# Front of a two-branch attention kernel: a third tile for branch A's outputs, two tiles for the query copies

## The chip, the cores and the metric

The kernel runs on one core of a Trainium2 chip. The metric is the device time of one execution in microseconds (us), the median over several runs. Engines are named as the profile names them: PE is TensorE (PEld its weight loads), ACT is ScalarE, DVE is VectorE, POOL is GpSimd, SP the engine that issues most DMAs here.

## The reference

Two attention branches over the same input x of 2048 rows and 512 columns, mixed row by row by a gate. Branch A is a sliding window of 8 positions with a step of 2, branch B full attention with one key and value head shared by 32 query heads of 16 columns.

```python
def _A_ref(x, wqkv, wo):          # H = 32, Dh = 16, W, dil = 8, 2
    qkv = (x @ wqkv).reshape(B, S, 3, H, Dh).transpose(2, 0, 3, 1, 4)
    q, k, v = qkv[0], qkv[1], qkv[2]
    idx = pos[:, None] - (jnp.arange(W) * dil)[None, :]
    logits = jnp.einsum("bhsd,bhswd->bhsw", q, kg) * scale   # kg, vg: rows idx of k, v
    attn = softmax(where(idx >= 0, logits, -1e9))
    return jnp.einsum("bhsw,bhswd->bhsd", attn, vg) ... @ wo

def _B_ref(x, wq, wk, wv, wo):
    q, k, v = heads(x @ wq), x @ wk, x @ wv
    p = softmax(jnp.einsum("bhqd,bkd->bhqk", q, k) * (Dh ** -0.5))
    return jnp.einsum("bhqk,bkd->bhqd", p, v) ... @ wo

g = sigmoid((x * gate_w).sum(-1, keepdims=True))
return g * _A_ref(...) + (1 - g) * _B_ref(...)
```

## The kernel before

**Stages.** The first 290 us are the front. It splits x and the weights into a high and a low part (`xh`, `xl`, `wqh`, `wql`, `wah`, `wal`), so that three products of reduced precision stand for one of full precision, and makes branch B's keys and queries and branch A's queries, keys and values. Then follow 16 units of branch B (4 blocks of 512 query rows by 8 groups of 4 heads, taken in 16 pairs), each over 16 key tiles: `exp_pair` makes scores and exponentials, `weighted` multiplies them with the values. Three output phases and a tail project both branches. Branch A's own arithmetic runs on POOL beside the units.

**Lumps.** The front's TensorE work is a list of lumps: query products m = 2 to 15, and 64 products (gg, j) of branch A, four column groups gg by 16 row tiles j. A lump is 12 products (4 chunks of the inner dimension by 3 parts), each cut into two matmuls of 64 rows (`h = slice(64 * b, ...)` in `mm`), one for the lower and one for the upper half of the array; two such matmuls run at once. The banks `fb[0]` to `fb[3]` take the lumps in turn (the last two go to `m1` and `po`).

**Between them** TensorE makes scores of branch B for the row maxima that the exponentials subtract. `fill_diff` (line 401) multiplies the queries with differences of keys (`diff_mm`, line 399) into a bank `pd0` or `pd1`; ACT copies it through a Relu into `dd` or `dd2` (line 411); `fill_sum` (line 419) makes plain scores into `m1` or `po`, and DVE adds the two and takes the maximum (line 423). A bank `pd` is free for the next difference once ACT has copied it.

**After a query lump** `queries_post` (line 217) has ACT copy the bank into `qraw` (line 223), and POOL then makes the high part `qhi` (line 230) and the low part `qlo` (line 231) from that copy. `queries_out` stores both to the scratch `qd` in HBM, and `stack` loads whole units of queries from there into a `qst` tile, both on SP's queue. `qraw` has one buffer in the pool `parts0`.

**After a lump of branch A** `a_post` (line 246) has ACT copy the bank into a stage tile (line 257), two row tiles j to a tile; when the second is in, SP stores the pair (384 KB) to the scratch `ad` (line 265), from where POOL's branch A loads it. With gg = 0 ACT also copies the values and the gate's column (line 259). The stage tiles are taken in turn from the list `stages`. A tile is added while the list has fewer than two or the key `"next"` is set; `done_mm` sets that key once, with the pool `third`, at the first lump of branch A, and the first `a_post` takes it out again. So the list ends with two tiles, `stage0` in the pool `third` and `stage1` in the pool `phase1`.

**What sets the order.** The program is one list of instructions written by Python; running clocks (`clk`) model each engine, `pick` and `front_stream` choose the next matmul by them, and `tasks` hold work with a due time (splits, stores, loads) that `run_tasks` issues when the modelled time is reached. The modelled clocks don't know which buffer an instruction writes: that an engine waits for a buffer is added by the framework, as a semaphore wait on the instruction. Each engine then runs its own instructions in this order, and SP issues its DMAs in this order.

**Memory.** `wkr` holds the key weights, read by `keys` (line 195) for the four key products at the start, in the pool `phase0`, which like `parts0` is given back when the first lump of branch A has begun (`done_mm`). `a_values` (line 595) is part of POOL's branch A: `av` holds a product for one window position, and `tr8`, `tr4`, `tr2` in `a_scores` hold the steps of a tree sum.

Of the kernel before, what the change touches and what calls it, by code (L numbers as in the profile page):

```python
# [6 lines left out]
F32 = mybir.dt.float32  # L7
# [6 lines left out]
P = 128  # L14
# [3 lines left out]
DH = 16  # L18
NJ = S // P
C = D // P  # L20
# [9 lines left out]
AG = 2  # L30
# [10 lines left out]
NH = NJ // 2  # L41
# [7 lines left out]
def gated_mix_kernel(ctx, tc, xt, wa, wk, wq, wo_a, wo_b, out):  # L49
# [36 lines left out]
    def after(eng, ready, dur):  # L86
        clk[eng] = max(clk[eng], ready) + dur
        return clk[eng]
# [4 lines left out]
    p0q = tc.alloc_tile_pool(name="parts0", bufs=1, side="right")  # L93
    p0 = tc.alloc_tile_pool(name="phase0", bufs=1, side="right")
# [3 lines left out]
    dd2 = p1.tile([P, 2, 512], F32, name="dd2")  # L98
    wqh = p0.tile([P, C, D], F32R, name="wqh")
    wql = p0.tile([P, C, D], F32R, name="wql")  # L100
    wkr = p0.tile([P, C, P], F32, name="wkr")
    wqr = [t[:, k].rearrange("p (c q) -> p c q", c=C) for t in (wq01, dd) for k in range(2)]
    waraw, wah, wal = {}, {}, {}
    GO = [0, GN + VN, 2 * GN + VN, 3 * GN + VN]
# [104 lines left out]
    def queries_out(m, hi, lo):  # L209
        qb, cc = divmod(m, NHG // 2)  # L210
        for s, src in enumerate((hi, lo)):
            nc.sync.dma_start(qd[s, :, qb, 8 * cc:8 * cc + 8, :], src.bitcast(F32))

    def parts_of():
        return p0q.tile([P, 512], F32R, name="qhi", bufs=3), p0q.tile([P, 512], F32R, name="qlo", bufs=2)

    def queries_post(m, bank, key, ups_at):

        nonlocal pool
        settle("rest", 0)  # L220
        own = p0q.tile([P, 512], F32, name="qraw", bufs=1)
        hi, lo = parts_of()
        got = nc.scalar.activation(own, bank, AF.Copy)
        at = after("act", clk["pe"] + T_LAT, 0.62)
        mark(got, at, ups_at)
        free[key] = at + 0.1

        def rest():
            nonlocal pool
            nc.gpsimd.tensor_copy(hi, own)  # L230
            nc.gpsimd.tensor_sub(lo, own, hi.bitcast(F32))
            pool = max(pool, 1e3 * at) + 2300
            queries_out(m, hi, lo)
            if m > 4 and m % 2 and len(stacked) < NB:
                stack(len(stacked))

        tasks.append((max(pool / 1e3, at), rest, (), "rest"))

    stage, stages, turns = {}, [], [0, 0]
# [6 lines left out]
    def a_post(gg, j, bank, key, ups_at):  # L246

        if j % 2 == 0:
            settle("store", 1)
            if len(stages) < 2 or "next" in stage:  # L250
                stages.append((stage.pop("next", None) or p1).tile([P, GC, 2, AN], F32, name=f"stage{len(stages)}"))
            stage["t"] = stages[turns[1] % len(stages)]
            turns[1] += 1
        st = stage["t"]
        end = gg == C - 1 and j == NJ - 1
        src = bank[:, :GN].rearrange("p (g n) -> p g n", g=GC)
        got = nc.vector.tensor_copy(st[:, :, 1, :], src) if end else nc.scalar.activation(st[:, :, j % 2, :], src, AF.Copy)
        if gg == 0:
            nc.scalar.activation(vst[:, j, 0:DH + 1], bank[:, GN:GN + DH + 1], AF.Copy)
        at = after("dve" if end else "act", clk["pe"] + T_LAT, 0.5 if gg else 0.7)  # L260
        mark(got, at, ups_at)
        free[key] = at + 0.1
        if j % 2 == 1:
            dst = ad[gg * GC:(gg + 1) * GC, HALO:, :].rearrange("g (p j) n -> p g (j n)", j=NJ)
            tasks.append((at + 0.3, lambda: nc.sync.dma_start(dst[:, :, (j - 1) * AN:(j + 1) * AN], st.rearrange("p g j n -> p g (j n)")), (), "store"))
        if j == NJ - 1:
            tasks.append((at + 1.0, whole, (gg,)))
# [21 lines left out]
    def stack(u):  # L289
        qb, hg = divmod(u, NHG)  # L290
        for b in range(2):
            hi, lo = (qd[s, :, qb, 4 * hg + 2 * b:4 * hg + 2 * b + 2, :].rearrange("d c n -> d (c n)") for s in range(2))
            ap = [list(x) for x in hi.ap]
            twice = bass.AP(tensor=hi.tensor, offset=hi.offset, ap=[ap[0], [0, 2]] + ap[1:])
            dst = qst[place(u)].rearrange("p c n -> p (c n)").bitcast(F32)
            nc.sync.dma_start(dst[64 * b:64 * b + 32], twice)
            nc.sync.dma_start(dst[64 * b + 32:64 * b + 48], lo)
        stacked.append(clk["pe"] + (6.8 if pe else 5.0))
# [11 lines left out]
    def mark(inst, end, up=None):  # L310
        marks.append((ups[0] if up is None else up, end, inst.ins.name))
# [220 lines left out]
    oa, p2, woh, wol, p1x = [], [], [], [], []  # L532
# [62 lines left out]
    def a_values(g, hf):  # L595
        lg, e = alog.pop(g), aext.pop(g)
        js = slice(NH * hf, NH * hf + NH)
        lgv = lg.rearrange("p w j h -> p w (j h)")
        nc.gpsimd.tensor_mul(asum[g], asum[g], gate[:, 0, js].unsqueeze(2).to_broadcast([P, NH, AG]))
        nc.gpsimd.tensor_mul(lgv, lgv, asum.pop(g).rearrange("p j h -> p (j h)").unsqueeze(1).to_broadcast([P, W, NH * AG]))  # L600
        yield 850
        ao = oa[g // 8][:, js, g % 8 * AC:(g % 8 + 1) * AC].rearrange("p j (h d) -> p j h d", d=DH)
        for w in range(W):
            o = HALO - DIL * w
            av = p2[0].tile([P, NH, AG, DH], F32, name="av", bufs=1) if w else ao
            nc.gpsimd.tensor_mul(av, e[:, o:o + NH, 2 * AC:].rearrange("p j (h d) -> p j h d", d=DH), lg[:, w].unsqueeze(3).to_broadcast([P, NH, AG, DH]))  # L606
            yield 730
            if w:
                nc.gpsimd.tensor_add(ao, ao, av)  # L609
                yield 830  # L610
# [311 lines left out]
    def settle(kind, n):  # L922
        for task in [t for t in tasks if t[3:] == (kind,)][:-n or None]:
            tasks.remove(task)
            task[1](*task[2])
# [52 lines left out]
    def work():  # L978
# [16 lines left out]
        def values(g, hf):  # L995
            while ("sum", g, hf) not in done:
                if summing:
                    yield lambda: ("exp",) + summing[0] in done
                    yield from sums()
                else:  # L1000
                    yield lambda: ("sum", g, hf) in done
            yield lambda: g < 8 or p2b
            yield from a_values(g, hf)
            if g == NAG - 1:
                done.add(hf)
# [118 lines left out]
    def done_mm(at):  # L1124
# [27 lines left out]
        if lump[0] == "q":  # L1152
            m = lump[1]
            queries_post(m, bank, key, ended_at.pop(x))
            ahead_wa(0, m - 4)
        else:
            gg, j = lump[1:]
            a_post(gg, j, bank, key, ended_at.pop(x))
            if gg + 1 < C:
                ahead_wa(gg + 1, j - 2)  # L1160
# [165 lines left out]
    for x in range(2):  # L1326
        js = slice(2 * x, 2 * x + 2)
        two = four[:, x]
        tt, own = two[:, 0].rearrange("p (b d) -> p b d", d=32), two[:, 1]
# [61 lines left out]
```

## Time and profile before

| | us |
|---|---|
| median of 3 runs (lowest, highest) | 1464.12 (1463.6, 1466.82) |
| the profiled execution | 1463.92 |
| its span, first to last instruction | 1462.1 |
| mean granted clock of TensorE | 0.999 |
| busy: PE, ACT, DVE, POOL | 1448.2, 1292.0, 1141.9, 954.6 |

A row of a timeline has the start and the length in us, the engine, the line, the operation and its tiles (out<-in, without buffer numbers), the shape, and in square brackets the idle time of the engine ahead of it and what ended it. A row of the table of waits has who waited for whom, the total in us, how many times, and the longest. A row of the chain of waits has start, length and what the chain went through. A row of the table by windows has the window, its length, the busy time (and instructions) of PE, PEld, DVE, ACT and POOL, the granted clock of TensorE, the share of the DMA engines and GB/s.

### The profile page before, as it was taken

What the parts mean: (1) busy time and instruction counts of PE and PEld (TensorE: products, weight loads), DVE (VectorE), ACT (ScalarE), POOL (GpSimd) and SP (SyncE); (2) the same over time, 40 slices, a digit from 0 to 9 for tenths busy, and PEclk for the clock granted to TensorE, in tenths of its full rate; (3) what the DMA queues carried; (4) which work ended last, traced back from release to release, by engine and by line L of the source; (5) the groups of instructions that cost most, each with busy time, mean ns of one, the idle gap of its engine ahead of it and who ended that gap; (6) DMA issues with size and microseconds to landing.
All of it is one profiled execution on the core that took longest, in us unless ns stands there. A gap on an engine that the chain in (4) does not pass through costs nothing.

```text
span 1462.1 us, 29622 instructions
## 1 busy us (share of the span) xinstructions
PE 1448.2 (99%) x10989; PEld 743.1 (51%) x10989; DVE 1141.9 (78%) x1857; ACT 1292.0 (88%) x1649; POOL 954.6 (65%) x1714
## 2 busy tenths in 40 slices
PE   9999999999999999999999999999999999999999
PEld 6899999833333333333333373333333743373335
DVE  6888888788887888888888876888888778778821
ACT  5788888699999999999999988999999889879994
POOL 6951888888979898898898897888881211130000
PEclk9999999999999999999999999999999999999999
DMA  6652442411202111012022020211200000000000
GB/s 225 171 159 72 146 129 89 136 49 41 79 12 79 47 44 68 31 39 78 17 74 72 13 93 8 82 42 42 71 12 13 27 16 1 2 31 1 1 2 29
DMA packets 45688, 85.70 MB, mean 59 GB/s; under 512 B 10400, under 2 KB 28248, under 8 KB 41448
## 3 DMA queue, kind: packets, MB, share of 16 engines
q1 hardware_dynamic: 38552, 45.21, 10.0%
q0 software_dynamic: 6560, 37.95, 7.8%
q8 instruction: 86, 1.41, 0.4%
q10 hardware_dynamic: 432, 0.66, 0.1%
q14 instruction: 58, 0.48, 0.1%
HBM read 57.97 MB, written 25.25 MB: 57 GB/s over the span
## 4 chain that ended last, share of the span: by engine, by line
PE 92%; POOL 2%; ACT 2%; DVE 1%; issue 1%; DMA 1%; SPq 0%; POOLq 0%; ACTq 0%; DVEq 0%
PE po L486 34%; PE pe L471 24%; PE pf L1109 9%; PE pm L328 8%; PE ps L328 5%; PE pe L803 5%; PE pd L399 3%; PE po L328 1%; PE pe L1320 1%; ACT pexp L477 1%; DMA ad<-stage 1%; POOL xl L82 1%; DVE mx L350 1%; DMA xraw<-xt 0%; PE pf L195 0%
## 5 line engine op out<-in xcount | busy, mean ns | idle before, releaser
L477 ACT ACTIVATE pexp<-pe 128x1024 f32<-128x1024 f32 x1021 | 983.4, 1023 | 64.4 <-PE pe L471 61.1
L350 DVE TENSOR_REDUCE mx<-pm 128x2 f32<-128x1024 f32 x470 | 574.0, 1221 | 178.1 <-PE pm L328 174.4
L486 PE MATMUL po<-pexp,vst 128*32 128x512 f32 x4096 | 546.4, 605 | 4.5 <-DVE mx L423 3.3
L471 PE MATMUL pe<-qst,kst 64*128 64x512 f32 x1914 | 492.6, 459 | 2.0 <-ACT pexp L477 2.0
L471 PEld LDWEIGHTS pe<-qst,kst 64*128 64x128 f32 x1914 | 193.5, 184 | 437.0 <-ACT pexp L477 408.6
L411 ACT ACTIVATE dd<-pd 128x512 f32<-128x512 f32 x384 | 224.5, 601 | 50.7 <-PE pd L399 24.7
L362 DVE TENSOR_REDUCE mx<-ps 128x1 f32<-128x512 f32 x309 | 209.8, 679 | 3.4 <-PE pe L803 2.0
L328 PE MATMUL ps<-kst,qst 62*128 62x512 f32 x475 | 194.2, 409 | 0.2
L549 POOL TENSOR_TENSOR pr<-aext 128x256 f32<-128x256 f32 x256 | 181.9, 740 | 4.2 <-DMA aext<-ad 4.0
L328 PE MATMUL pm<-kst,qst 62*128 62x512 f32 x880 | 178.7, 397 | 0.5 <-ACT pexp L477 0.2
L609 POOL TENSOR_TENSOR oa<-oa,av 128x256 f32<-128x256 f32 x224 | 164.1, 733 | 15.8
L486 PEld LDWEIGHTS po<-pexp,vst 128*32 128x32 f32 x4096 | 80.6, 108 | 171.7 <-issue 157.2
L423 DVE CUSTOM_DVE_ANT_0 dd<-ps,dd 128x512 f32<-128x512 f32 x193 | 133.0, 689 | 25.8 <-PE ps L328 7.8
L423 DVE CUSTOM_DVE_ANT_0 dd<-po,dd 128x512 f32<-128x512 f32 x191 | 131.6, 689 | 22.6 <-PE po L328 10.2
L1109 PE MATMUL pf<-wal,xh 64*128 64x384 f32 (+1 forms) x496 | 148.3, 337 | 0.0
L399 PE MATMUL pd<-kd,qst 62*128 62x512 f32 x372 | 146.4, 398 | 1.7 <-ACT dd L411 1.7
L606 POOL TENSOR_TENSOR av<-aext,lg 128x256 f32<-128x256 f32 x224 | 139.4, 622 | 12.6
L1109 PE MATMUL pf<-wah,xh 64*128 64x384 f32 (+1 forms) x496 | 145.7, 338 | 0.0
L1109 PE MATMUL pf<-wah,xl 64*128 64x384 f32 (+1 forms) x496 | 142.3, 337 | 0.0
L328 PEld LDWEIGHTS ps<-kst,qst 62*128 62x128 f32 x475 | 87.8, 185 | 33.7 <-DVE mx L362 25.6
L513 POOL TENSOR_TENSOR rl<-rl,gate_t 128x16 f32<-128x16 f32 x31 | 7.1, 230 | 143.3 <-DVE rl L506 143.1
L1109 PEld LDWEIGHTS pf<-wal,xh 64*128 64x128 f32 x496 | 90.7, 186 | 0.3
(210 smaller groups left out, 1817.6 us busy)
## 6 DMA issues: line engine op xcount, KB each, us to landing
aext<-ad POOLq DMA_DIRECT2D x32, 1056.0 KB, 5.4
ad<-stage SPq DMA_DIRECT2D x32, 384.0 KB
qst<-qd SPq DMA_DIRECT2D x60, 128.0 KB
xraw<-xt SPq DMA_DIRECT2D x16, 256.0 KB
qd<-qhi SPq DMA_DIRECT2D x16, 256.0 KB
qd<-qlo SPq DMA_DIRECT2D x16, 256.0 KB
qst<-qd SPq DMA_DIRECT2D x60, 64.0 KB
qst<-ml SPq DMA_DIRECT2D x212, 2.0 KB
```

The lines of the kernel that those rows point to most:

```text
L328: nc.tensor.matmul(dst, qst[place(v)][b:b + 62, pr, t * P:(t + 1) * P], kst[b:b + 62, kc * 512:(kc + 1) * 512], start=True, stop=True)
L350: got = nc.vector.tensor_reduce(m[:, :, pr, t, kc], dst, AX.X, ALU.max)
L362: got = nc.vector.tensor_reduce(m[:, odd, pr, t, kc:kc + 1], dst, AX.X, ALU.max)
L399: nc.tensor.matmul(dst, qst[place(v)][b:b + 62, pr, t * P:(t + 1) * P], kd[0][b:b + 62, kc // 2, :], start=True, stop=True)
L411: got = nc.scalar.activation(held[b][k], dst, AF.Relu)
L423: got = nc.vector.tensor_tensor_reduce(held[b][k], dst, held[b][k], 1.0, -FMAX, ALU.add, ALU.max, m[:, b, pr, t, kc:kc + 1])
L471: nc.tensor.matmul(bank[:, odd, :], kst[b:b + 64, kt * P:(kt + 1) * P], qst[place(u)][b:b + 64, pr, :], start=True, stop=True)
L477: got = nc.scalar.activation(e, bank, AF.Exp, scale=SCALE)
L486: nc.tensor.matmul(po[32 * i:32 * i + 32, :], vst[:, kt, :], pexp[s, i // 2][:, i % 2, :], start=(kt == 0), stop=(kt == NJ - 1))
L549: nc.gpsimd.tensor_mul(pr[:, k], q, e[:, o:o + NH, AC:2 * AC])
L609: nc.gpsimd.tensor_add(ao, ao, av)
L1109: inst = nc.tensor.matmul(home(x)[0][:, :n], l[h], r[h], start=(i == 0 and b == 0), stop=(i == 3 * C - 1 and b == 1))
```

## The change

Three things change place in memory. The list `stages` takes a third tile, `stage2`, in the pool `phase1` (the condition with `"next"` is replaced by a plain count). The copies of even query products go to a tile of their own, `qraw2`, in the memory of `wkr`; the odd ones stay in `qraw`. And `av` shares the memory of `tr4`.

```diff
-    wkr = p0.tile([P, C, P], F32, name="wkr")
+    wkr = p0.tile([P, C, P], F32, name="wkr", tag="wkr", bufs=1)
...
-        own = p0q.tile([P, 512], F32, name="qraw", bufs=1)
+        own = p0q.tile([P, 512], F32, name="qraw", bufs=1) if m % 2 else p0.tile([P, 512], F32, name="qraw2", tag="wkr", bufs=1)
...
-            if len(stages) < 2 or "next" in stage:
+            if len(stages) < 3:
                 stages.append((stage.pop("next", None) or p1).tile([P, GC, 2, AN], F32, name=f"stage{len(stages)}"))
...
-            av = p2[0].tile([P, NH, AG, DH], F32, name="av", bufs=1) if w else ao
+            av = p2[0].tile([P, NH, AG, DH], F32, name="av", tag="tr4", bufs=1) if w else ao
```

Every engine has the same instructions in the same places before and after; what changes is the tile that some of them write, and what they wait for. Two places on ACT's queue show it. In these rows a name carries its number, `dd` and `dd2` are the Relu copies, `pf` the lumps' banks, `DMAHW` a DMA's semaphore, `Pool` POOL's.

The query copies of m = 3 (in `qraw`) and m = 4, with the Relu copies between them, on ACT. Before:

```order
L411 ACTIVATE dd2_122<-pd1_93 128x512 [waits PE_49]
L223 ACTIVATE qraw_426<-pf1_98 128x512 [waits PE_49,Activation_49,Pool_49]
L411 ACTIVATE dd_86<-pd0_92 128x512 [waits PE_49]
L411 ACTIVATE dd_86<-pd1_93 128x512 [waits DVE_49,PE_49]
L411 ACTIVATE dd2_122<-pd0_92 128x512 [waits PE_49]
L411 ACTIVATE dd2_122<-pd1_93 128x512 [waits DVE_49,PE_49]
L411 ACTIVATE dd_86<-pd0_92 128x512 [waits DVE_49,PE_49]
L411 ACTIVATE dd_86<-pd1_93 128x512 [waits DVE_49,PE_49]
L223 ACTIVATE qraw_482<-pf2_99 128x512 [waits PE_49,Activation_49,Pool_49]
```

And after, at the same place on ACT:

```order
L411 ACTIVATE dd2_122<-pd1_93 128x512 [waits PE_49]
L223 ACTIVATE qraw_426<-pf1_98 128x512 [waits PE_49]
L411 ACTIVATE dd_86<-pd0_92 128x512 [waits PE_49]
L411 ACTIVATE dd_86<-pd1_93 128x512 [waits DVE_49,PE_49]
L411 ACTIVATE dd2_122<-pd0_92 128x512 [waits PE_49]
L411 ACTIVATE dd2_122<-pd1_93 128x512 [waits DVE_49,PE_49]
L411 ACTIVATE dd_86<-pd0_92 128x512 [waits DVE_49,PE_49]
L411 ACTIVATE dd_86<-pd1_93 128x512 [waits DVE_49,PE_49]
L223 ACTIVATE qraw2_482<-pf2_99 128x512 [waits PE_49,Activation_49,Pool_49]
```

The copy of m = 3 no longer waits for POOL; that of m = 4 still does, for POOL's work on m = 2 in place of m = 3.

The stage copies of j = 3 and j = 4 of the first column group on ACT. Before:

```order
L257 ACTIVATE stage1_1303<-pf1_98 128x4x96 [waits PE_49]
L259 ACTIVATE vst_72<-pf1_98 128x17
L411 ACTIVATE dd2_122<-pd1_93 128x512 [waits DVE_49,PE_49]
L411 ACTIVATE dd_86<-pd0_92 128x512 [waits DVE_49,PE_49]
L411 ACTIVATE dd_86<-pd1_93 128x512 [waits DVE_49,PE_49]
L411 ACTIVATE dd2_122<-pd0_92 128x512 [waits DVE_49,PE_49]
L257 ACTIVATE stage0_1207<-pf2_99 128x4x96 [waits DMAHW5_49,PE_49,Activation_49]
```

And after, at the same place on ACT:

```order
L257 ACTIVATE stage1_1303<-pf1_98 128x4x96 [waits PE_49]
L259 ACTIVATE vst_72<-pf1_98 128x17
L411 ACTIVATE dd2_122<-pd1_93 128x512 [waits DVE_49,PE_49]
L411 ACTIVATE dd_86<-pd0_92 128x512 [waits DVE_49,PE_49]
L411 ACTIVATE dd_86<-pd1_93 128x512 [waits DVE_49,PE_49]
L411 ACTIVATE dd2_122<-pd0_92 128x512 [waits DVE_49,PE_49]
L257 ACTIVATE stage2_1391<-pf2_99 128x4x96 [waits PE_49]
```

The copy of j = 4 waits for the store of j = 0, 1 before, and for its product alone after. Every later pair waits for the store of three pairs before in place of two. Beyond that, the first stage copy (j = 0) gets a wait for POOL's `qlo` of m = 14, since `stage0` lies in memory that `qraw2`'s pool gives back, and one load of `qstx` on SP's queue a wait for ACT's copy of m = 14. No row of `av` gets a wait.

## The prediction

> **What bounds the kernel now.** I read the page's busy times and chain of waits first, then the front alone (0 to 290 us, all that the change touches), and there who waited for whom.
>
> ```profile
> PE 1448.2 (99%) x10989; PEld 743.1 (51%) x10989; DVE 1141.9 (78%) x1857; ACT 1292.0 (88%) x1649; POOL 954.6 (65%) x1714
> PE 92%; POOL 2%; ACT 2%; DVE 1%; issue 1%; DMA 1%; SPq 0%; POOLq 0%; ACTq 0%; DVEq 0%
> ...
> ACT stage L257 <- DMA ad<-stage: 4.5, 2, 3.0
> ...
> ACT qraw L223 <- POOL qlo L231: 4.4, 4, 2.5
> ...
> PE pd L399 <- ACT dd L411: 1.7, 4, 0.9
> ```
>
> The chain is TensorE for 92%: whatever lets its queue run on is worth its whole length, and an ACT wait is worth only what reaches TensorE through it. ACT waits 4.5 us (two times) for a stage buffer's store and 4.4 us (four times) for POOL to finish with the query copy: 8.9 us in all. Behind them stand the Relu copies `dd` of line 411, and the difference matmuls of line 399 need the bank that such a copy empties. TensorE is shown idle there for 1.7 us in four places. A stall costs more than its idle time, since the modelled ends of matmuls cover part of it, so below I take it from start to start, against the usual step from one pair of half-array matmuls to the next: 0.235 us at 512 columns (63.15 to 63.39 in the rows below), and by the columns 0.18 us for the A products with their 384 or 402.
>
> **The query copies.** With one `qraw`, the copy of query product m waits until POOL has split m-1; now it waits for m-2. The first two rows are ACT's at m=3, the others TensorE's.
>
> ```profile
> 38.80 0.60 ACT L223 ACTIVATE qraw<-pf 128x512 f32<-128x512 f32 x1 [2.49 <-POOL qlo L231]
> 39.29 3.70 ACT L411 ACTIVATE dd<-pd 128x512 f32<-128x512 f32 x6
> ...
> 37.59 0.39 PE L1109 MATMUL pf<-xh,wql 64*128 64x512 f32 x1
> 39.22 0.39 PE L328 MATMUL po<-kst,qst 62*128 62x512 f32 x1
> 39.94 0.50 PE L399 MATMUL pd<-kd,qst 62*128 62x512 f32 x1 [0.33 <-ACT dd L411]
> 40.27 0.40 PE L1109 MATMUL pf<-xl,wqh 64*128 64x512 f32 x1
> ```
>
> The last matmul into m=3's bank ends at 37.59 + 0.39 = 37.98, so the copy can start 0.8 us earlier and the next `dd` can end near 39.1 instead of 39.9. TensorE wants it at 39.22 + 0.235 = 39.46, so the stall goes whole: (39.94 - 39.22 - 0.235) + (40.27 - 39.94 - 0.235) = 0.58 us; the second bracket is the slow restart behind it. The same at m=5 and m=8:
>
> ```profile
> 47.45 0.60 ACT L223 ACTIVATE qraw<-pf 128x512 f32<-128x512 f32 x1 [0.74 <-POOL qlo L231]
> 48.02 0.39 PE L1109 MATMUL pf<-xh,wqh 64*128 64x512 f32 x1
> 48.58 0.49 PE L399 MATMUL pd<-kd,qst 62*128 62x512 f32 x1 [0.16 <-ACT dd L411]
> 48.92 0.40 PE L1109 MATMUL pf<-xh,wql 64*128 64x512 f32 x1
> ...
> 61.67 0.60 ACT L223 ACTIVATE qraw<-pf 128x512 f32<-128x512 f32 x1 [0.99 <-POOL qlo L231]
> 62.09 0.39 PE L1109 MATMUL pf<-xh,wqh 64*128 64x512 f32 x2
> 62.81 0.50 PE L399 MATMUL pd<-kd,qst 62*128 62x512 f32 x1 [0.33 <-ACT dd L411]
> 63.15 0.40 PE L1109 MATMUL pf<-xl,wqh 64*128 64x512 f32 x2
> 63.39 0.40 PE L1109 MATMUL pf<-xh,wql 64*128 64x512 f32 x2
> ```
>
> They give 0.325 + 0.105 = 0.43 and 0.485 + 0.105 = 0.59 us. The fourth wait, 4.4 - 2.49 - 0.74 - 0.99 = 0.2 us, has no TensorE stall behind it: nothing. Together 1.60 us. POOL's own work, two instructions and two stores a product, is untouched.
>
> **The third stage buffer.** With two, pair j/2 of the A products waits for the store of two pairs before; now of three. The profile shows it bind twice. First at j=4; the first row is of the chain of waits, the next three ACT's, the last three TensorE's:
>
> ```profile
> 102.93 3.23 DMA ad<-stage
> ...
> 104.15 0.60 ACT L411 ACTIVATE dd<-pd 128x512 f32<-128x512 f32 x1 [0.16 <-PE pf L1109]
> 106.27 0.49 ACT L257 ACTIVATE stage<-pf 128x384 f32<-128x384 f32 x1 [1.52 <-DMA ad<-stage]
> 106.72 2.34 ACT L411 ACTIVATE dd<-pd 128x512 f32<-128x512 f32 x4
> ...
> 106.13 0.34 PE L1109 MATMUL pf<-wah,xl 64*128 64x402 f32 x1
> 107.37 0.49 PE L399 MATMUL pd<-kd,qst 62*128 62x512 f32 x1 [0.91 <-ACT dd L411]
> 107.67 0.34 PE L1109 MATMUL pf<-wal,xh 64*128 64x402 f32 x1
> ```
>
> ACT is free at 104.75, and the store issued at 102.93 frees the buffer at 106.16. With a fresh buffer the copy starts some 1.5 us earlier and the `dd` that TensorE misses ends near 105.7, before it is wanted (106.31): (107.37 - 106.13 - 0.18) + (107.67 - 107.37 - 0.18) = 1.18 us. Then at j=14, the seam to the exponentials; the first two rows are SP's, the third of the chain, the rest TensorE's and ACT's:
>
> ```profile
> 268.26 0.36 SPq L265 DMA_DIRECT2D ad<-stage  x1
> 274.28 3.26 SPq L459 DMA_DIRECT2D qst<-ml  x5
> 277.64 6.82 DMA ad<-stage
> ...
> 282.10 0.33 PE L1109 MATMUL ps<-wah,xl 64*128 64x384 f32 x1
> 284.00 0.41 PE L471 MATMUL pe<-qst,kst 64*128 64x512 f32 x2
> 284.56 0.49 ACT L257 ACTIVATE stage<-ps 128x384 f32<-128x384 f32 x1 [3.01 <-DMA ad<-stage]
> 284.95 2.85 ACT L477 ACTIVATE pexp<-pe 128x1024 f32<-128x1024 f32 x3
> ```
>
> The store of j=10, 11 is held in SP's queue behind five small transfers and then takes 6.82 us. With three buffers the copy waits for the store issued at 268.26, long landed, and starts at 282.45. The exponentials behind it then wait for their scores alone, 284.00 + 0.41 = 284.41: (284.95 - 284.43) = 0.52 us. From there ACT and TensorE hand each other tiles, so both move up. The other 30 writes of a pair are relaxed too, but wait for nothing now.
>
> The Trainium skill, page "SBUF — State Buffer", section "The DMA setup-cost knee", gives a transfer 2 us plus its bytes at 436 GB/s: for 384 KB an estimate of 2.9 us. By that rule a store is long done when its buffer comes round, and this part would win nothing. The trace agrees on the lone transfer (3.23 us), and disagrees on the other (6.82 us).
>
> **What else moves.** No engine's order changes. The copy `qraw2` lies where the key weights were; their last readers stand ahead of m=2's own products in TensorE's queue, and the copy waits for those anyway: nothing. `av` in `tr4`'s memory has only POOL on both sides, in order, with no wait added: nothing; a wait there would cost POOL alone, which is busy for 65% of the span. Two waits are new. The first stage copy now waits for POOL's split of m=14, and one `qstx` load on SP for ACT's copy of it, with the shift rows and stage stores queued behind.
>
> ```profile
> 86.94 1.30 POOL L231 TENSOR_TENSOR qlo<-qraw,qhi 128x512 fp32r<-128x512 f32 x1
> 92.07 0.49 ACT L257 ACTIVATE stage<-pf 128x384 f32<-128x384 f32 x1
> ...
> 80.36 1.30 POOL L231 TENSOR_TENSOR qlo<-qraw,qhi 128x512 fp32r<-128x512 f32 x1 [2.03 <-DMA qd<-qlo]
> 82.20 0.90 POOL L141 TENSOR_TENSOR wal<-waraw,wah 128x402 fp32r<-128x402 f32 x1
> ```
>
> The split ends at 88.24, 3.83 us ahead of the stage copy; TensorE brings that forward by 1.60 us at most, which leaves 2.2. The copy that SP waits for is older still than that split, which reads it. I take nothing; the bounds are nothing and the rival below.
>
> **The sum.** 1.60 + 1.18 + 0.52 = 3.30 us. The profiled execution took 1463.92 us, 1.8 more than its span (1462.1) and 0.2 less than the median 1464.12: the same within the spread of 1463.6 to 1466.82. Forecast 1464.12 - 3.30 = 1460.8 us. Its own range: without the four restarts (0.4) and half the seam (0.25) 2.65 us, 1461.5; with one more stall of the size of those at the copies (0.5), which no row ties to them, 3.8 us, 1460.3.
>
> **The rivals.** I count 0.2% as no change (2.93 us, which a measurement of this kernel can hardly tell): 1461.2 is the line, inside the forecast's range.
>
> *Two buffers were enough.* A lone store takes 3.23 us, and two products fill a buffer in (104.75 - 92.07) / 2 = 6.3, so a store issued in time is never waited for. If what held ACT at the two places comes earlier by no more than now, late issue and shared transfer included, only the queries' 1.60 us are won: 1462.5. That is where the rule of the page above leads. Against it are the two rows that name the store of two turns back. 8%, no change.
>
> *Given back to POOL and SP.* POOL stands at 80.36 for a store held in SP's queue, which needn't come earlier. If TensorE, 1.60 us ahead, then waited for POOL's last weight split, that gain is gone: 1.70 us left, 1462.4. Against it: that split ends at 82.20 + 0.90 = 83.1, five us and more ahead of the products that read it, and no row shows TensorE waiting for POOL here. 10%, no change.
>
> *All that ACT waited comes through*, 8.9 us: 1455.2. Against it: TensorE had work in most of that time. 4%, faster.
>
> *The clock's windows.*
>
> ```profile
> 880.00:885.00 5.00, 2.75 (x13) 0.86 (x14) 1.90 (x4) 1.86 (x3) 3.44 (x9) 0.70 0.15 53
> 882.42 1.94 PE L486 MATMUL po<-pexp,vst 128*32 128x512 f32 x8 [2.25 <-DVE mx L423]
> ```
>
> The first row is of a table by windows (its granted clock is the 0.70), the second TensorE's. After an idle of 2.25 us at the end of an output phase TensorE ran slowed: 5 x (1 - 0.70) = 1.5 us of clock lost. Work that comes at other moments can meet one more such loss (1462.3, no change) or be spared this one (1459.3, faster): 8% each, since nothing in the front speaks for either. The Trainium skill, page "TensorE: Matmul & The Clock Gate", section "What's actually happening", has the clock halve after an idle window of some 3.4 us, in windows that run free of the program. The trace's idle is shorter than that, so there the trace decides; that the windows run free would make both signs alike, and the stalls removed here, 0.91 us idle at most, are far too short to matter to the clock, as the trace has it too.
>
> *Slower: the new wait on the first stage copy binds.* Place: ACT at 92 us, with `dd` behind it and TensorE behind that. It decides once POOL's split of m=14 is over 2.2 us late, and each further us costs up to one. To end over 1467.05 it must eat 3.30 and 2.93 more, so POOL must be 8.4 us late, four waits like that at 80.36; at 8.9 us it gives 1467.5. Against it: POOL reads a copy that comes earlier too. 4%. That the change doesn't make a third buffer is ruled out: the order shows `stage2`.
>
> **How the numbers follow.** The forecast has 58%; of its range 2.65 to 3.8 us some three quarters lie beyond 2.93, 45%, and 13% are no change. Faster: 45 + 4 + 8 = 57%. No change: 13 + 8 + 10 + 8 = 39%. Slower: 4%. The range 1459.0 to 1462.7 takes in the forecast, both clock cases and the two cases of lost gain, 92%, of which I count off a tenth for the sizes.
>
> **What would show it.** Right: no row of ACT at line 257 waiting for `ad<-stage` and none at 223 for `qlo`; no start-to-start gap over 0.4 us before line 399 near 39, 48, 62 and 106; the first triple of exponentials 3.3 us earlier than 284.95; the rest of the span as long as before. Wrong: these gaps gone but the triple less than 2.6 us earlier (a stall further on took it), or a new wait of ACT for POOL at the first stage copy.

## The result and the profile after

| | before | after |
|---|---|---|
| median, us | 1465.54 (1463.13 to 1467.26, 17 executions) | 1460.67 (1459.3 to 1462.9, 17 executions) |
| span of the profiled execution, us | 1462.1 | 1458.8 |
| after / before | | 0.9974 (95% interval 0.9967 to 0.9981) |

The change makes the kernel faster by 0.26%, 3.8 us of 1465.54 (2.8 to 4.8); the two medians alone differ by 4.87. The prediction had 3.30 us, from 1464.12 to 1460.8; with more executions the median of the kernel before rose to 1465.54, and the two profiled spans differ by 3.3.

The page after: its span, its busy times, the shares of the chain that ended last.

```profile
span 1458.8 us, 29619 instructions
...
PE 1446.8 (99%) x10989; PEld 743.8 (51%) x10989; DVE 1141.6 (78%) x1857; ACT 1291.9 (89%) x1649; POOL 954.3 (65%) x1714
...
PE 95%; DVE 1%; POOL 1%; ACT 1%; DMA 1%; issue 0%; SPq 0%; POOLq 0%; ACTq 0%; DVEq 0%
```

No engine works less: ACT's 1291.9 us are the 1292.0 of before. Only order in time has changed, and TensorE's share of the chain went from 92% to 95%. Who waited for whom in the first 520 us (total us, times, longest):

```profile
ACT dd L411 <- PE pd L399: 12.7, 42, 0.6
...
ACT stage L257 <- PE pf L1109: 4.6, 4, 2.2
...
POOL qlo L231 <- DMA qd<-qlo: 3.7, 2, 3.2
...
ACT qraw L223 <- PE pf L1109: 3.1, 2, 1.7
```

The two waits of before are gone: a stage copy waits for its product alone, no longer for a store, and a query copy for its product, no longer for POOL. ACT now idles for TensorE, which costs nothing. POOL waits longer for the stores of `qlo` (3.7 us in two waits, 2.0 in one before), as the rival "given back to POOL and SP" had it, but there is no row of TensorE waiting for POOL behind it.

Now the places. First ACT's copies at m=3, at the first stage tile and at j=4, then the seam with the single exponential ahead of it; then TensorE where it stood at 39.94; then POOL's split of m=14.

```profile
38.32 0.60 ACT L223 ACTIVATE qraw<-pf 128x512 f32<-128x512 f32 x1 [1.72 <-PE pf L1109]
...
90.61 0.49 ACT L257 ACTIVATE stage<-pf 128x384 f32<-128x384 f32 x1
...
103.16 0.48 ACT L257 ACTIVATE stage<-pf 128x384 f32<-128x384 f32 x1
...
277.53 1.03 ACT L477 ACTIVATE pexp<-pe 128x1024 f32<-128x1024 f32 x1 [1.01 <-PE pe L471]
279.47 0.49 ACT L257 ACTIVATE stage<-ps 128x384 f32<-128x384 f32 x1 [0.92 <-PE ps L1109]
281.45 2.86 ACT L477 ACTIVATE pexp<-pe 128x1024 f32<-128x1024 f32 x3 [1.49 <-PE pe L471]
...
39.51 0.39 PE L328 MATMUL po<-kst,qst 62*128 62x512 f32 x1
39.72 0.40 PE L399 MATMUL pd<-kd,qst 62*128 62x512 f32 x1
39.74 0.39 PE L1109 MATMUL pf<-xh,wql 64*128 64x512 f32 x1
...
85.86 1.30 POOL L231 TENSOR_TENSOR qlo<-qraw,qhi 128x512 fp32r<-128x512 f32 x1 [0.50 <-DMA qd<-qlo]
```

At 39.51 to 39.74 the steps are the usual 0.2, where before there was a hole of 0.7. The stage copy at j=4 moved from 106.27 to 103.16. The triple of exponentials starts at 281.45, 3.50 us ahead of the 284.95 of before. The split of m=14 ends at 85.86 + 1.30 = 87.16, 3.45 us ahead of the first stage copy that now waits for it.

Two executions do not begin alike: the loads at the start end a little sooner or later. A fair zero is TensorE's first product for the row maxima (line 328), here of before (with ACT's first single exponential behind it) and then of after:

```profile
25.11 0.49 PE L328 MATMUL ps<-kst,qst 62*128 62x512 f32 x1
...
280.53 1.03 ACT L477 ACTIVATE pexp<-pe 128x1024 f32<-128x1024 f32 x1 [1.01 <-PE pe L471]
```

```profile
25.40 0.50 PE L328 MATMUL ps<-kst,qst 62*128 62x512 f32 x1
```

Counted from there, the change is worth 3.79 us at the triple: 284.95 - 25.11 = 259.84 before, 281.45 - 25.40 = 256.05 after. That the spans differ by the forecast's 3.30 is luck: the first fill itself comes 0.29 us later after the change, and what follows the triple is 0.20 us longer (1458.8 - 281.45 against 1462.1 - 284.95). The table has the same three marks for the kernels below, each the start of a row less the start of this one.

| us from the first fill | first stage copy | stage copy j=4 | first triple of exponentials |
|---|---|---|---|
| before | 66.96 | 81.16 | 259.84 |
| after | 65.21 | 77.76 | 256.05 |
| query copies only | 65.13 | 79.40 | 258.61 |
| third stage tile only | 66.98 | 79.58 | 257.98 |
| memory move only | 66.95 | 81.48 | 260.36 |
| two tiles, stores by POOL and ACT | 65.21 | 77.78 | 256.14 |
| base of the last four runs | 67.22 | 81.97 | 260.45 |

Before, memory move and base have the same two stage tiles and one query buffer, and their triples stand up to 0.6 us apart: a smaller difference between two single traces may be chance.

### The profile page after: what moved, and what is told of

It reads as the page before. It is cut to its first block, busy times and chain, and to the rows that moved or that the text cites. A ratio compares the mean times of both kernels' runs of the same rounds, so it can differ in the third digit from the quotient of the medians.

```text
span 1458.8 us, 29619 instructions
## 1 busy us (share of the span) xinstructions
PE 1446.8 (99%) x10989; PEld 743.8 (51%) x10989; DVE 1141.6 (78%) x1857; ACT 1291.9 (89%) x1649; POOL 954.3 (65%) x1714
## 4 chain that ended last, share of the span: by engine, by line
PE 95%; DVE 1%; POOL 1%; ACT 1%; DMA 1%; issue 0%; SPq 0%; POOLq 0%; ACTq 0%; DVEq 0%
PE po L486 34%; PE pe L471 24%; PE pf L1109 11%; PE pm L328 8%; PE ps L328 6%; PE pe L803 5%; PE pd L399 3%; PE po L328 1%; PE pf L195 1%; PE pe L1320 1%; ACT pexp L477 1%; DVE mx L350 1%; POOL tr L555 0%; DMA xraw<-xt 0%; POOL pr L549 0%
## 5 line engine op out<-in xcount | busy, mean ns | idle before, releaser
L1109 PE MATMUL pf<-wah,xl 64*128 64x384 f32 (+1 forms) x496 | 147.0, 337 | 0.0
L1109 PEld LDWEIGHTS pf<-wah,xl 64*128 64x128 f32 x496 | 91.2, 186 | 0.4
```

The source lines that it names most:

```text
L1109: inst = nc.tensor.matmul(home(x)[0][:, :n], l[h], r[h], start=(i == 0 and b == 0), stop=(i == 3 * C - 1 and b == 1))
```

## The experiments

**The two parts alone.** The query copies without the third tile:

```diff
-    wkr = p0.tile([P, C, P], F32, name="wkr")
+    wkr = p0.tile([P, C, P], F32, name="wkr", tag="wkr", bufs=1)
...
-        own = p0q.tile([P, 512], F32, name="qraw", bufs=1)
+        own = p0q.tile([P, 512], F32, name="qraw", bufs=1) if m % 2 else p0.tile([P, 512], F32, name="qraw2", tag="wkr", bufs=1)
```

> Only the query copies get their second buffer; the stage tiles stay two. Theory of the prediction (the two parts add): the start-to-start gaps near 39, 48 and 62 us go, 1.60 us; the stage copy at j=4 still waits for its store (about 1.5 us, TensorE's gap of 1.18 us near 107 stays) and at j=14 too, since the stores come earlier together with the products. First triple of exponentials near 283.3, ratio 0.9989. Rival, two buffers were enough: with the products earlier the store waits go or cost TensorE nothing, and the ratio is that of the whole change, 0.9974. Second rival, eaten by the store: the store doesn't come earlier, the wait at j=4 grows by 1.6 us, and the ratio is 1.000.

Measured: 1463.91 us against 1465.53, ratio 0.9989 (0.998 to 0.9998). In its trace ACT and TensorE at j=4 and ACT at the seam:

```profile
104.52 0.49 ACT L257 ACTIVATE stage<-pf 128x384 f32<-128x384 f32 x1 [1.59 <-DMA ad<-stage]
...
105.62 0.49 PE L399 MATMUL pd<-kd,qst 62*128 62x512 f32 x1 [0.99 <-ACT dd L411]
...
283.34 0.49 ACT L257 ACTIVATE stage<-ps 128x384 f32<-128x384 f32 x1 [2.93 <-PE pe L471]
283.73 1.94 ACT L477 ACTIVATE pexp<-pe 128x1024 f32<-128x1024 f32 x2
```

The store's wait at j=4 stands (1.59 us, 1.52 before), so there the store came earlier together with the products: neither "two buffers were enough" nor "eaten by the store". The seam stands too. The page names TensorE as what ended ACT's wait of 2.93 us there, but a wait for several things is put down to the one that came last by the profile, and the triple follows the first single exponential (279.38) by 4.35 us, as before by 4.42 and after by 3.92. The copy also starts as long after its store left SP as before (276.41 to 283.34, 6.93 us; before 277.64 to 284.56, 6.92): it is still the store that sets it.

Further on a part of the gain is eaten, though. Here are a store on SP's queue, ACT's stage copy at j=12 of the second column group, which by the turn of the two tiles writes the tile of that store, and TensorE behind it:

```profile
176.03 0.37 SPq L265 DMA_DIRECT2D ad<-stage  x1
...
179.25 0.49 ACT L257 ACTIVATE stage<-pf 128x384 f32<-128x384 f32 x1 [0.62 <-PE pd L399]
...
180.29 0.49 PE L399 MATMUL pd<-kd,qst 62*128 62x512 f32 x1 [0.17 <-ACT dd L411]
```

The copy starts 3.22 us after the store of two pairs before left SP, as long as the lone store took; in the kernel before it is 3.13 us (177.10 to 180.23) and no wait is shown. So in this execution two tiles were just short here too (inferred from these times; the row names TensorE); the other three traces with the query copies and two tiles lose nothing at this place. The copies behind it are 1.28 us ahead of the kernel before in place of 1.72, and at the triple 1.23 us are left.

The third stage tile without the query copies:

```diff
-            if len(stages) < 2 or "next" in stage:
+            if len(stages) < 3:
...
-            av = p2[0].tile([P, NH, AG, DH], F32, name="av", bufs=1) if w else ao
+            av = p2[0].tile([P, NH, AG, DH], F32, name="av", tag="tr4", bufs=1) if w else ao
```

> Only the third stage tile (and the value products' memory that makes room for it); the query copies keep one buffer. Theory of the prediction: the three gaps near 39.9, 48.6 and 62.8 us stay, ACT waits 4.4 us in all for POOL at the query copy, no stage copy waits; 1.18 + 0.52 = 1.70 us less, ratio 0.9988, first triple of exponentials near 283.2. Rival, the parts overlap: the third tile is worth something only once the copies have moved, ratio 1.000. Second rival, the seam is worth more than 0.52 us since TensorE's queue behind it moves too: over 2.5 us less, ratio 0.998 or below.

Measured: 1462.39 us, ratio 0.9976 (0.9968 to 0.9985), 3.5 us, twice what was expected and outside the interval. But its trace shows what the theory has:

```profile
39.12 0.60 ACT L223 ACTIVATE qraw<-pf 128x512 f32<-128x512 f32 x1 [2.48 <-POOL qlo L231]
...
40.25 0.50 PE L399 MATMUL pd<-kd,qst 62*128 62x512 f32 x1 [0.32 <-ACT dd L411]
...
105.01 0.49 ACT L257 ACTIVATE stage<-pf 128x384 f32<-128x384 f32 x1
...
283.41 2.85 ACT L477 ACTIVATE pexp<-pe 128x1024 f32<-128x1024 f32 x3 [1.48 <-PE pe L471]
```

The waits at the query copies stand, those at the stage copies are gone, and the triple is 1.86 us earlier from the first fill. So some 1.6 us of the 3.5 were won behind the front, where the change does nothing. The windows of 5 us around the first output phase's end (busy time and instructions of PE, PEld, DVE, ACT and POOL, then the granted clock, DMA share, GB/s) show what differs there, first of the third tile alone, then of the query copies alone:

```profile
880.00:885.00 5.00, 2.80 (x20) 1.01 (x24) 3.13 (x5) 2.91 (x5) 4.07 (x9) 1.00 0.16 56
885.00:890.00 5.00, 5.00 (x41) 1.91 (x34) 3.33 (x4) 4.62 (x6) 2.82 (x4) 1.00 0.00 0
```

```profile
880.00:885.00 5.00, 3.47 (x20) 1.41 (x24) 2.77 (x5) 2.60 (x3) 4.35 (x9) 0.72 0.16 56
885.00:890.00 5.00, 5.00 (x25) 1.57 (x27) 2.00 (x3) 3.08 (x4) 2.50 (x4) 0.59 0.00 0
```

Both kernels have TensorE idle for the same 2.25 us there, and then the one keeps its full clock and the other loses 5 x (0.28 + 0.41) = 3.45 us of it. The profiled executions of the two kernels compared met it once each, first of before (behind the window with 0.70), then of after:

```profile
885.00:890.00 5.00, 4.57 (x33) 1.69 (x31) 2.83 (x3) 4.70 (x5) 3.66 (x5) 0.95 0.01 3
```

```profile
875.00:880.00 5.00, 2.75 (x21) 1.50 (x21) 3.21 (x8) 2.90 (x4) 3.34 (x5) 0.90 0.01 1
880.00:885.00 5.00, 4.62 (x28) 1.64 (x22) 1.23 (x1) 2.86 (x3) 4.79 (x10) 0.76 0.16 56
```

That is 5 x (0.30 + 0.05) = 1.75 us of clock lost before and 5 x (0.10 + 0.24) = 1.70 after. The mean granted clock of every execution points the same way: at 1.000 the third tile alone has a median of 1461.66 us (seven of eleven executions) and the kernel before one of 1463.88 (six of 33), 2.2 us apart and not 3.5. Why this kernel kept its clock more often isn't shown. The clock differs between executions, and the part that it takes can't be told from the change in eleven executions. This is why the last four runs below were made.

**The memory move.** The `av` line of the diff above alone.

> Only the value products of branch A move into the partial sums' memory; no buffer is added. Theory of the prediction: nothing, ratio 1.000 within 0.0007, POOL's busy time the same within 1 us. Rival, POOL waits for its own partial sums there or runs slower on those addresses: POOL's sums reach the output later, ratio above 1.001.

Measured: 1464.76 us against 1465.53, ratio 0.9998 (0.9989 to 1.0006); POOL busy 954.4 us, 954.6 before. As expected: nothing.

**What the third tile pays for.** Two tiles, the query copies as changed, and the two stores for which a copy waited sent by another queue than SP's. At first both by ACT:

```diff
-            tasks.append((at + 0.3, lambda: nc.sync.dma_start(dst[...], st...), (), "store"))
+            tasks.append((at + 0.3, lambda: (nc.scalar if (gg, j) in ((0, 1), (C - 1, 11)) else nc.sync).dma_start(dst[...], st...), (), "store"))
```

> Query copies in two buffers, two stage tiles only, and the two stores for which a stage copy waited (rows j=0,1 of the first group and j=10,11 of the last) issued from ACT's queue right behind their copies, not from SP's. Theory (a store's late issue is what the third tile pays for): no stage copy waits, the triple of exponentials stands where the whole change has it (281.45) within 0.4 us, ratio 0.9970 to 0.9980. Rival (a pair of tiles is too few for the transfer itself): the stage copies still wait, ratio 0.9989 as with the query copies alone. Second rival: the issue on ACT costs ACT more than it frees, and a stall of TensorE stands near 96 or 270 us in its place.

Measured: ratio 1.0002 (0.9993 to 1.0011): all gain gone, also that of the query copies. No stage copy waits for a store any more, as the theory has it, but the second rival holds too. ACT's queue with its issue (ACTq), TensorE, and one window of the table by stretches:

```profile
98.25 0.39 ACTq L265 DMA_DIRECT2D ad<-stage  x1
98.73 1.09 ACT L411 ACTIVATE dd<-pd 128x512 f32<-128x512 f32 x2 [3.10 <-DMA qstx<-qd]
...
99.38 0.50 PE L399 MATMUL pd<-kd,qst 62*128 62x512 f32 x1 [2.25 <-ACT dd L411]
...
100.00:105.00 5.00, 5.00 (x39) 5.00 (x37) 2.72 (x8) 3.14 (x9) 0.33 (x1) 0.66 0.27 85
```

By the profile the issue itself stood until a load of `qstx`, an earlier transfer, had landed: ACT 3.10 us, TensorE 2.25 behind it, and then the clock was granted at 0.66 for 5 us (the last row, a window). In SP's queue the store left later still (102.93 in the kernel before), but ACT's own work went on meanwhile. So the first store was then sent by POOL, the other left on ACT, where its wait held nobody:

```diff
+            ... {(0, 1): nc.gpsimd, (C - 1, 11): nc.scalar}.get((gg, j), nc.sync).dma_start(...)
```

> As the run before with two stage tiles and a timely issue, but the first of the two stores goes out from POOL's queue, since on ACT's queue the issue itself stood 3.10 us behind a load of qstx and TensorE 2.25 us behind ACT; the second stays on ACT's queue, where it held nobody. Theory (late issue in SP's queue is all that the third tile pays for): no stage copy waits, no new gap of TensorE near 96 us, the first triple of exponentials as far from the first fill as with the whole change (230.65 us, within 0.4), ratio 0.9967 to 0.9981. Rival: the issue is late on any queue, since it has to wait for an earlier transfer's end wherever it stands; the stage copy at j=4 waits again or POOL's weight splits are late, ratio 0.9989 or above.

Measured: 1461.93 us against 1465.87, ratio 0.9973 (0.9963 to 0.9983), the whole change's ratio, with two tiles. (The 230.65 us of the expectation take off the 25.40 twice; the mark that it means is the table's 256.05.) POOL's issue, then ACT at j=4, ACT's issue of the second store, and the seam:

```profile
94.04 0.82 POOL L265 DMA_DIRECT2D ad<-stage  x1 [1.20 <-ACT vst L259]
...
102.69 0.48 ACT L257 ACTIVATE stage<-pf 128x384 f32<-128x384 f32 x1
...
272.58 0.39 ACTq L265 DMA_DIRECT2D ad<-stage  x1
...
281.05 1.94 ACT L477 ACTIVATE pexp<-pe 128x1024 f32<-128x1024 f32 x2 [1.49 <-PE pe L471]
```

The stores leave at 94.04 and 272.58, where SP sent them at 102.93 and 277.64 in the kernel before, and j=4 and the triple stand within 0.1 us of the whole change's marks (77.78 and 256.14 in the table). So two tiles were enough for the transfers; what the third buys is time for a store that is held in SP's queue.

**The slower rival, brought about.** POOL's copy to `qhi` at m=14 is made fourteen times, in the whole change and in the kernel before:

```diff
-            nc.gpsimd.tensor_copy(hi, own)
+            [nc.gpsimd.tensor_copy(hi, own) for _ in range(14 if m == 14 else 1)]
```

> The whole change, and POOL makes the copy to qhi of m=14 fourteen times in place of once (13 more at 0.69 us; the split ends near 95.7 us in place of 87.16). Theory: this is the slower rival's case made on purpose: the first stage copy, at 90.61 without it, waits for that split to its end, 5.1 us late, and TensorE loses 4 to 5 us there; later SP's queue holds the first store longer, up to 2 us more at j=6. Ratio 1.0000 to 1.0015. Rival: the first stage copy's memory isn't what it waits for and nothing happens at 90.6 us, ratio 0.9974.

> The kernel before with the same fourteen copies at m=14, the split ending near 96.8 us. Theory: with one query buffer the copy of m=15, at 89.5 us without it, waits for that split, 7.3 us late, so TensorE loses 6 to 7 us, and the store of j=0,1 is as late as the products: ratio 1.0040 to 1.0055. So the second query buffer moves POOL's lateness from m=15's copy to the first stage copy and makes it 2 us cheaper. Rival: with the new wait of the change gone the lateness costs nothing here, ratio 1.000.

Measured: 1.0015 (1.0006 to 1.0023) and 1.0044 (1.0031 to 1.0057). ACT's and TensorE's rows, of the change and then of before:

```profile
95.78 0.49 ACT L257 ACTIVATE stage<-pf 128x384 f32<-128x384 f32 x1 [4.93 <-POOL qlo L231]
...
96.89 0.79 PE L399 MATMUL pd<-kd,qst 62*128 62x512 f32 x1 [4.33 <-ACT dd L411]
```

```profile
97.14 0.60 ACT L223 ACTIVATE qraw<-pf 128x512 f32<-128x512 f32 x1 [7.44 <-POOL qlo L231]
...
98.28 0.79 PE L399 MATMUL pd<-kd,qst 62*128 62x512 f32 x1 [6.89 <-ACT dd L411]
```

The new wait is real: with POOL's split some 8.6 us late it holds ACT for 4.93 us and TensorE for 4.33. But the buffer that brings it takes away a dearer one: before, about the same lateness holds the copy of m=15 for 7.44 us and TensorE for 6.89. From the first fill the triple is 6.20 us later with the change (262.25 against 256.05) and 9.11 without it (268.95 against 259.84). So in the front the change makes the kernel less, not more, sensitive to POOL. The whole times don't show it: the lateness costs 1.0015 - 0.9974 = 0.0041 with the change and 0.0044 without, the same within the intervals. What follows the triple differs by the clock again: in the profiled executions 5.1 us of it were lost there with the change and none without.

**A version that beats both, and a steady base.** What the whole change still has to lose stands at the ends of the output phases. Its rows of VectorE and TensorE there:

```profile
876.04 0.41 PE L328 MATMUL po<-kst,qst 62*128 62x512 f32 x1
...
877.84 0.69 DVE L686 COPY two<-pe 128x512 f32<-128x512 f32 x1 [1.36 <-ACT two L685]
878.45 0.68 DVE L423 CUSTOM_DVE_ANT_0 dd<-po,dd 128x512 f32<-128x512 f32 x1
...
879.28 1.93 PE L486 MATMUL po<-pexp,vst 128*32 128x512 f32 x8 [2.25 <-DVE mx L423]
```

The sum of line 423 empties the bank `po` for which TensorE waits; its input was there at 876.04 + 0.41 = 876.45, but it stands in VectorE's queue behind half a copy (line 686) that waits for ACT's half. So that half was put behind the sums:

```diff
             nc.scalar.activation(two[:, 0], eb[k][:, 0, :], AF.Copy)
-            nc.vector.tensor_copy(two[:, 1], eb[k][:, 1, :])
+            owed.append(lambda: nc.vector.tensor_copy(two[:, 1], eb[k][:, 1, :]))
...
+        while owed:
+            owed.pop(0)()
         plain_todo()
```

(The addition and the store that need it follow it in the same list.)

> The whole change, and at the end of each output phase VectorE's half of the last copy (line 686, which waits 1.36 us for ACT's half) is put behind the sums that empty the bank po, not ahead of them. Theory: TensorE's wait of 2.25 us at 879 for VectorE goes to under 0.6, the one of 1.1 us near 1300 too, and with them the slowed clock behind the first: 2 to 4 us less than the whole change, ratio 0.9945 to 0.9965. Rival: ACT's exponentials set the end there too, as at the phase near 1165 where TensorE waits for them already, and the weighted sums start no sooner: ratio 0.9974.

Measured: 1456.94 us (1456.48 to 1457.46) against 1465.87, ratio 0.9937 (0.9925 to 0.9949), more than the 0.9945 expected at the most; the same kernel gave 0.9948 later (last row of the table below).

```profile
877.13 0.69 DVE L423 CUSTOM_DVE_ANT_0 dd<-po,dd 128x512 f32<-128x512 f32 x1
...
878.37 0.69 DVE L686 COPY two<-pe 128x512 f32<-128x512 f32 x1 [0.54 <-ACT two L685]
...
877.98 1.06 PE L486 MATMUL po<-pexp,vst 128*32 128x512 f32 x8 [0.41 <-ACT pexp L477]
...
880.00:885.00 5.00, 4.34 (x33) 1.71 (x31) 3.05 (x3) 4.62 (x6) 4.86 (x10) 1.00 0.16 56
```

TensorE's idle there is 0.41 us, now for ACT; the one of 1.1 us at the last output phase is gone, and the clock (the last row, its 1.00) holds. And the five executions lie within 1.0 us, where those of the kernels without this edit lie 3.2 us or more apart in all runs but one (the kernel before with POOL held, 1.4). All 28 executions of the five kernels with this edit have a mean granted clock of 1.000, those without it 0.995 to 1.000. On this base the two parts were measured again, each with that edit and nothing else:

> The kernel before with only the later place of VectorE's half of the last copy, which took TensorE's idle of 2.25 us and the slowed clock behind it out of the run before. It is the base for the three runs with it. Theory: 3.3 us of idle less, and the slowed clock's one or two us: 1460.5 to 1462 us, executions within about 1.5 us of each other. Rival (the clock slows on its own, without that idle): they stay spread over 4 us as those of the kernel before.

> The query copies' second buffer alone, on that base. Theory: 1.75 us less than the base, as the first stage copy stood earlier in the trace (the prediction says 1.60), that is 0.9988 of it; rival: nothing, as the trace's first exponentials stood only 1.2 us earlier with this part alone.

> The third stage tile alone, on that base. Theory (two stalls, and the clock's chances made the rest of the 3.5 us that this part won alone): 1.9 us less than the base, as the triple of exponentials stood earlier in the trace (the prediction says 1.70). Rival: the third tile is worth 3.5 us by itself, and the two parts overlap.

> Both parts on that base, the kernel of the run b2 again. Theory (the parts add): 3.4 to 3.8 us less than the base. Rival (they overlap): no less than the third tile alone.

| with VectorE's half behind the sums | median, us (executions) | less than the base | ratio to the kernel before |
|---|---|---|---|
| base: neither part | 1460.62 (1459.86 to 1461.66, 8) | | 0.9968 (0.9958 to 0.9979) |
| query copies | 1458.47 (1458.1 to 1459.21, 5) | 2.15 | 0.9959 (0.9946 to 0.9971) |
| third stage tile | 1458.73 (1458.33 to 1459.22, 5) | 1.89 | 0.9959 (0.9947 to 0.9972) |
| both | 1457.04 (1456.51 to 1457.59, 5) | 3.58 | 0.9948 (0.9935 to 0.996) |

The rival that gives the third tile 3.5 us by itself falls. The parts make 4.04 us apart and 3.58 together; with spreads of one to two us that is no sure overlap. (By the ratios, whose intervals reach some 1.8 us to each side, the steps are 1.3, 1.3 and 2.9 us.) The one edit behind the front is worth about as much as the change studied here: 1465.15 - 1460.62 = 4.5 us, by its ratio 3.1 to 6.2, against 2.8 to 4.8.

## Why the prediction was right, point by point

- *The query copies, 1.60 us.* Right. All three holes are gone. From the first fill the first stage copy is 1.75 us earlier with the change and 1.83 with this part alone; on the steady base the part is worth 2.15. Alone it keeps only 1.23 us up to the triple of its profiled execution, since the stage copy near 179 us takes some back. The prediction doesn't have that; with the third tile nothing is lost there, and the trace of this part on the steady base loses nothing there either. The fourth wait (0.17 us) was counted at nothing, and the small rest of 0.15 can't be told from the spread.
- *The stage buffer at j=4, 1.18 us.* Right. With the third tile alone the next pair's first copy (j=6) is 1.10 us earlier from the first fill, 85.88 against 86.98; with the change the second half of its 2.94 us there, less the 1.75 of the queries, is 1.19. The stall itself isn't one size: ACT waited 1.52 us in the profiled execution before, 1.59 with the query copies alone, 1.87 with the memory move and 2.07 in the steady base, since the store lands sooner or later.
- *The seam, 0.52 us.* Right: from the first single exponential to the triple 4.42 us before and 3.92 after, 0.50. (The prediction sets 284.43 where its row gives 284.41, which changes nothing.)
- *The sum, 3.30 us.* Right, and a little small: the steady base gives 3.58, the ratio 3.8 (2.8 to 4.8), the triple from the first fill 3.79. Of this the named places make 1.75 + 1.19 + 0.50 = 3.44. The other 0.35 come between j=6 and the first single exponential (2.94 us ahead at the one, 255.42 - 252.13 = 3.29 at the other), where the prediction has nothing. Most of it is one step of 0.26 us between two stage copies (207.56 to 211.10 before, 204.80 to 208.08 after) that the third tile alone has too; no stage copy is shown waiting there, and the cause stays open. In other executions the stall at j=4 was longer than in the profiled one of before, which can add to the ratio; that isn't shown.
- *Why the third tile is worth anything.* The prediction said that the store is held in SP's queue and that a lone store takes 3.23 us, and set "two buffers were enough" against it. That rival falls: the third tile alone is worth 1.89 us on the steady base. Issued by other queues, two tiles give the whole gain. The rule that the prediction cited from the Trainium skill, page "SBUF — State Buffer", section "The DMA setup-cost knee", was thus no reason against the gain: it speaks of a transfer that has been issued, and what was late was the issue. The transfer of 6.82 us that disagreed with it is no accident: at the same place the chains of three other kernels with two tiles have 6.59 (the base), 6.89 (memory move) and 6.91 us (before with POOL held). What makes it so long there wasn't tried.
- *Given back to POOL and SP.* POOL did wait longer for its stores, and nobody waited for POOL, so the rival falls.
- *All that ACT waited comes through, 8.9 us.* It doesn't: at the same copies ACT now waits for TensorE (1.72 us at m=3).
- *The slower rival.* The mechanism is real. The point from which it decides was put too early: the change left 3.45 us of room, not 2.2, because POOL's split moves forward with the copy that it reads.
- *The clock's windows.* The rival's mechanism is real, and its size was off. It was counted at one loss more or less of 1.5 us. The same idle of 2.25 us cost nothing in one profiled execution and 3.45 us of clock in another. Of this, about half becomes time: from the triple to the span's end it is 1459.9 - 283.41 = 1176.5 us with the third tile alone and 1462.1 - 283.73 = 1178.4 with the query copies alone; the memory move, with 5.15 us of clock lost, has 1465.8 - 286.24 = 1179.6. It didn't decide the change, since before and after lost about as much in their profiled executions (1.75 and 1.70 us), but it made one part look like 3.5 us.

## What to carry to other kernels

A stall of a helper engine is worth what comes through at the engine that bounds, measured from start to start there; added up that way, five stalls of half a microsecond to one gave the result within a fifth. Before a buffer is added for a transfer that lands late, look when it was issued: a store that stands in a queue behind other transfers wants another queue, and one whose issue itself must wait wants a queue that has nothing urgent behind it. When the parts of a change don't add up, look for an idle place elsewhere whose cost changes from execution to execution, take it out of all versions, and measure again.

## What the runs showed of the hardware

- After the same idle of TensorE of 2.25 us the granted clock in the next 10 us was 1.00 throughout (third tile alone), 0.70 and then 0.95 (the kernel before) or 0.72 and then 0.59 (query copies alone). The Trainium skill, page "TensorE: Matmul & The Clock Gate", section "What's actually happening", has a gate that looks at the idle in windows which run free of the program; that the same idle meets it now so, now so agrees with this, but the idle here is shorter than the 3.4 us that the page asks for. With the idle cut to some 0.4 us there, the profiled executions of all five such runs show a full clock at that place. The 2.25 us of the store issued by ACT, at another place of the program, were followed by 0.66 for 5 us.
- By the profile the issue of a store on ACT's queue waited 3.10 us for an earlier transfer to land; the same store issued by POOL left at 94.04 after a wait of 1.20 us for ACT's copies. What of this wait is the kernel's own semaphores and what the chip was not tried apart.
